# Two of four long blocks take 128 + 32 rows in the expert part of a top-k attention and mixture kernel

## The chip, the cores and the metric

The kernel runs on one core of one Trainium2 chip. Its time is the device time of one execution in microseconds. It was run three times for the figures below. The engines are TensorE (PE in the profile, its weight loads PEld), VectorE (DVE), ScalarE (ACT), GpSimd (POOL) and SyncE (SP), which issues most DMA transfers.

## The reference

Attention with top-k selection, then a mixture of experts in which each token goes to one expert and none is dropped. All numbers are fp32.

```python
# q, k, v: batch 8, heads 8, 576 tokens, head size 64; top_k = 32
scores = scale * np.matmul(q, k.transpose(0, 1, 3, 2))
kth = np.partition(scores, -top_k, axis=-1)[..., -top_k:-top_k + 1]
scores = np.where(scores >= kth, scores, -1000000000.0)
attn = softmax(scores)                     # with 1e-09 added to the sum
x = (attn @ v), laid out as (8 * 576, 8 * 64)          # 4608 x 512

logits = x @ w_gate                        # 512 x 8
expert_idx = np.argmax(logits, axis=1)
gate_w = softmax(logits) at expert_idx
# for each of the 8 experts e, with the rows that chose it:
y = np.maximum(rows @ w1[e], 0.0) @ w2[e]  # w1: 512 x 1024, w2: 1024 x 512
out = gate_w[:, None] * y                  # in the order of the tokens
```

The inputs are drawn with a fixed seed. Computed through the reference, the eight experts get 620, 519, 615, 513, 642, 507, 554 and 638 rows.

## The kernel before

The work goes batch by batch (8 batches of 576 tokens). In each, the attention of all heads is computed, the gate picks an expert for each token, and an indirect DMA (line 591) scatters the finished rows into `x_rows` in DRAM, where each expert has a region of its own. In between, the kernel takes *blocks* of rows of one expert through the two layers. Until the last batch these are full blocks of 128 rows; they are cut in pieces that are laid between the attention's instructions.

**The last part.** When the last batch is scattered, the rest is known: some full blocks and one remainder of each expert. What follows has a fixed length, written into the program: `SURE` = 2 blocks of 128 rows that are certain to be full, then `HALVES` = 4 *long* blocks, then `PLAIN` = 4 blocks of 128 rows. A long block takes a full block of an expert together with the first 64 rows (`ST`) behind it, the expert's remainder if it is 64 or less. So an expert's last full block and its short remainder share one loading of the weights, 2 MB for w1 and 2 MB for w2. Which expert a block is for is data: the program reads expert and row from a table.

**The table.** `counted` (line 699) works out for each expert the number of full blocks and a flag `half` for a remainder of at most 64. The first table (`table`, line 621) fills the two `SURE` slots. Then `end_table` (line 712) fills the long slots and the plain ones; what is left over sets `rest_i` and `rare`, which open a branch at the end of the program with spare blocks. All of that is VectorE work on one partition, on 1 to 200 numbers at a time. It uses `wTt` as scratch space. The long slots (`slot_long`) are a slice of `slot_last`. Behind the tables `fill_up` (line 606) reads each expert's end (`ends`, line 609) and writes 128 blank rows behind it (line 613), four from SP and four from GpSimd.

**The order of the work.** In the last part the instructions of PE, ACT and DVE stand in the order in which the Python code emits them. SP's queue runs in order too. Per block it holds: a read of the table and the load of the rows (`load_rows`, line 798), for a long block the load of the extra rows (`load_half`, line 812), then w1 (line 790) and w2 (line 792). At most two blocks are loaded ahead; w1 and w2 have two buffers each, so a load of w1 waits until PE has done with w1 of two blocks before.

**A long block** (`long_block`, line 872) does this on PE:

- `turned` transposes the 128 rows and the 64 rows (line 828); ACT copies both into `xT`, 4 x 192 columns (line 829).
- First layer (line 885): 8 x 4 matmuls with 128x128 weights and 192 moving columns; ACT applies the relu to four outputs at once, 768 columns (line 891).
- Between the two layers the next block's rows are transposed.
- Second layer (line 906): 8 steps of 4 matmuls with 192 columns; ACT copies the sum (line 913).
- `last` turns the result back (line 921), in two parts, 128 and 64 rows. It is put into the middle of the next block's first layer. ACT scales by the gate (line 925) and GpSimd stores the rows by an indirect DMA (line 858).

A plain block (`block`) has 32 matmuls with 128 columns in the first layer (line 949) and 8 with 512 columns in the second (line 966). The width of a long block's tiles is the constant `LONG = P + ST`, used in `spare_room` and `long_block`.

Of the kernel before, what the change touches and what calls it, by code (L numbers as in the profile page):

```python
# [9 lines left out]
F32 = mybir.dt.float32  # L10
# [34 lines left out]
def kernel(  # L45
# [82 lines left out]
    LONG = P + ST  # L128
# [95 lines left out]
    slot_long = slot_last[:, 0, NSLOT + SOON - 3 * E:].rearrange("o (i e) -> o i e", i=3)  # L224
    assert LAST - SURE <= NSLOT + SOON - 3 * E
# [473 lines left out]
    def counted():  # L699

        sm = k.small
        full, ci = sm.tile([1, E], F32, name="full"), sm.tile([1, E], I32, name="ci")
        half = wTt[0:1, 0:E]
        for to, more in ((half, P - 1), (full, ST - 1)):
            nc.vector.tensor_scalar_add(to, run[0:1, :], float(more))
            nc.vector.tensor_copy(ci, to)
            nc.vector.tensor_single_scalar(ci, ci, 7, op=ALU.arith_shift_right)
            nc.vector.tensor_copy(to, ci)
        nc.vector.tensor_tensor(half, half, full, op=ALU.subtract)
        return half, full  # L710

    def end_table(slot_i, slot_l, n, half, full):
# [4 lines left out]
        hupto, at = wTt[0:1, 3 * E:4 * E + 1], wTt[0:1, 5 * E:5 * E + NSLOT]  # L717
        long_f = wTt[0:1, 6 * E + NSLOT:9 * E + NSLOT].rearrange("o (i e) -> o i e", i=3)
# [6 lines left out]
        def looked_up(to, what, last):  # L725
            v.tensor_tensor(some[:, 0:E - 1], what[:, 1:E], what[:, 0:E - 1], op=ALU.subtract)
            v.tensor_tensor(past[:, E:2 * E, :], past[:, 0:E, :], _ins(some[:, :], 1, E), op=ALU.mult)
            v.tensor_reduce(to, past[:, E:2 * E, :], axis=AX.X, op=ALU.add)
            v.tensor_scalar(to, to, what[:, 0:1], None, ALU.add)

        def steps():
# [7 lines left out]
            v.tensor_tensor_scan(hupto[:, 1:], ones[0:1, 0:E], half, 0.0, op0=ALU.mult, op1=ALU.add)  # L739
            v.tensor_scalar(take, hupto[:, 1:], float(HALVES), None, ALU.is_le)  # L740
            v.tensor_tensor(take, take, half, op=ALU.mult)
            v.tensor_tensor(take, take, left, op=ALU.min)
            v.tensor_tensor(left, left, take, op=ALU.subtract)
# [5 lines left out]
            v.tensor_scalar(at[:, extra], slots[:, 0:HALVES], hupto[:, E:E + 1], float(EMPTY), ALU.is_lt, ALU.mult)  # L749
            v.tensor_tensor(at[:, extra], at[:, extra], slots[:, PLAIN:PLAIN + HALVES], op=ALU.add)  # L750
            v.tensor_scalar(at[:, extra], at[:, extra], hupto[:, E:E + 1], None, ALU.subtract)
# [12 lines left out]
            v.tensor_tensor(past[:, 0:E, :], _inner(slots[:, 0:E], E), _ins(hupto[:, 1:], 1, E), op=ALU.is_ge)  # L764
            v.tensor_reduce(long_f[:, 0, :], past[:, 0:E, :], axis=AX.X, op=ALU.add)
# [12 lines left out]
            v.tensor_scalar(some[:, 0:1], hupto[:, E:], float(HALVES), float(PLAIN + HALVES), ALU.min, ALU.subtract)  # L778
            v.tensor_tensor(some[:, 0:1], some[:, 0:1], upto[:, E:], op=ALU.add)
            v.tensor_scalar(some[:, 1:2], hupto[:, E:], float(-HALVES), 0.0, ALU.add, ALU.max)  # L780
# [27 lines left out]
    def load_half(n, piece):  # L808
        r = nc.sync.value_load(piece, min_val=0, max_val=EMPTY)
        room = k.att.tile([P, 2, S], F32, name="w", bufs=3)[:, :, :].rearrange("p m k -> p (m k)")  # L810
        n.half = room[:, 0:XW].rearrange("p (o w) -> p o w", o=1)
        got = nc.sync.dma_start(n.half[0:ST], xv[0:ST, bass.ds(r, 1), :]).ins
        for put in scattered:
            tc.add_manual_dep(got, put.name, WAIT)
        fetched.append(got)
        return n
# [4 lines left out]
    def turned(n):  # L821

        if hasattr(n, "half"):
            n.xT = spare_room(DT)
            for x, first, rows in ((n.x, 0, P), (n.half, P, ST)):
                ps = k.ps_m.tile([P, DT, P], F32, name="xtp", tag="m")
                for dt in range(DT):
                    nc.tensor.transpose(ps[:, dt, 0:rows], x[0:rows, 0, dt * P:(dt + 1) * P], ident[0:rows, 0:rows])
                due.append(("xT", lambda ps=ps, first=first, rows=rows: nc.scalar.copy(
                    n.xT[:, :, first:first + rows], ps[:, :, 0:rows]  # L830
                )))
            return
        if k.apart:
            ps = bank("xtp")[:, :].rearrange("p (t r) -> p t r", t=DT)
        else:
            ps = k.ps_m.tile([P, DT, P], F32, name="xtp", tag="m")
        for dt in range(DT):
            nc.tensor.transpose(ps[:, dt, :], n.x[:, 0, dt * P:(dt + 1) * P], ident)
        n.xT = k.mlp.tile([P, DT, P], F32, name="xTs")
        due.append(("xT", lambda: nc.scalar.copy(n.xT, ps)))  # L840
# [3 lines left out]
    def spare_room(n):  # L844
        flat = k.att.tile([P, 2, 2, HF], F32, name="s", bufs=4)[:, :, :, :].rearrange("p m j k -> p (m j k)")
        return flat[:, 0:n * LONG].rearrange("p (n r) -> p n r", r=LONG)
# [25 lines left out]
    def long_block(n, following):  # L872
# [6 lines left out]
        for half in range(2):  # L879
            ph = k.ps_s.tile([P, 2, SM], F32, name="sc")  # L880
            for f in range(FT // 2):
                fc = half * (FT // 2) + f
                to = ph[:, f // 2, f % 2 * LONG:(f % 2 + 1) * LONG]
                for dt in range(DT):
                    nc.tensor.matmul(
                        to, n.w1[:, 0, dt, fc * P:(fc + 1) * P], n.xT[:, dt, :],
                        start=(dt == 0), stop=(dt == DT - 1),
                    )
                if f == FT // 2 - 1:
                    hT.append(spare_room(FT // 2))  # L890
                    due.append((f"h{half}", lambda ph=ph, h=hT[half]: nc.scalar.activation(
                        h.rearrange("p (b f) r -> p b (f r)", b=2), ph[:, :, 0:2 * LONG], AF.Relu
                    )))
                yield
            if not half:
                finish()
# [4 lines left out]
        for step in range(2 * DT):  # L901
            odd, half, b = step // 4, step // 2 % 2, step % 2
            dc = 2 * b + odd
            to = pT[:, b, odd * LONG:(odd + 1) * LONG]
# [7 lines left out]
        yT = spare_room(DT)  # L912
        due.append(("y", lambda: nc.scalar.copy(
            yT.rearrange("p (b c) r -> p b (c r)", b=2), pT[:, :, 0:2 * LONG]
        )))

        def last():
            for x, first, rows in ((n.x, 0, P), (n.half, P, ST)):
# [75 lines left out]
    with fast:  # L994
# [26 lines left out]
        def ahead():  # L1021
            while waiting and len(loaded) < 2:
# [3 lines left out]
                elif isinstance(piece, list):  # L1026
                    rows_in = load_half(load_rows(SimpleNamespace(), piece[0]), piece[1])
# [53 lines left out]
        def ending(b, u):  # L1081
# [59 lines left out]
            if b == B - 1:  # L1141
                scatter(KC)
                slot_i = k.small.tile([1, 2, NSLOT], I32, name="slot_i")
                half, full = counted()
# [5 lines left out]
            if new:  # L1150
                if b == B - 1:
                    slot_i = slot_last
                    steps = end_table(slot_i, slot_long, new, half, full)
# [9 lines left out]
            if b == B - 1:  # L1163
                spare.extend(coming[PLAIN:])
                del coming[PLAIN:]
                longs = [[slot_long[0:1, i, j:j + 1] for i in range(3)] for j in range(E)]
                spare.extend((expert, half) for expert, half, _ in longs[HALVES:])
                coming[0:0] = [(expert, [full, half]) for expert, half, full in longs[:HALVES]]
# [272 lines left out]
```

## Time and profile before

| | |
|---|---|
| median of three runs | 1299.48 us (1299.31 to 1300.81) |
| the profiled execution | 1294.12 us |
| its span | 1292.5 us |
| mean granted TensorE clock | 0.97 |
| PE busy | 1185.8 us, 92% |
| DVE busy | 1057.5 us, 82% |
| ACT busy | 934.1 us, 72% |
| POOL busy | 730.1 us, 56% |
| 1075 to 1275 us: PE busy | 25.00 of 25 us in each of eight stretches |
| L885, 128x192 matmuls | 256 records, 42.8 us |
| L906, 128x192 matmuls | 256 records, 42.6 us |

The page of the profile gives each engine's busy time and a row of 40 slices of 32.3 us, each digit the busy share in tenths. The timeline lists instructions in order of time: start, duration, engine, line, operation, the tiles written and read, the form, and how many stand in a row. A PE record is given as weights and moving columns (128*128 128x192). Durations of PE records overlap, since matmuls are pipelined. Windows give busy times of all engines in a stretch. "SPq" are the issues of DMA transfers on SP's queue. Times are counted from the start of the span.

### The profile page before, as it was taken

What the parts mean: (1) busy time and instruction counts of PE and PEld (TensorE: products, weight loads), DVE (VectorE), ACT (ScalarE), POOL (GpSimd) and SP (SyncE); (2) the same over time, 40 slices, a digit from 0 to 9 for tenths busy, and PEclk for the clock granted to TensorE, in tenths of its full rate; (3) what the DMA queues carried; (4) which work ended last, traced back from release to release, by engine and by line L of the source; (5) the groups of instructions that cost most, each with busy time, mean ns of one, the idle gap of its engine ahead of it and who ended that gap; (6) DMA issues with size and microseconds to landing.
All of it is one profiled execution on the core that took longest, in us unless ns stands there. A gap on an engine that the chain in (4) does not pass through costs nothing. (4 is left out here: it accounts for less than half of the span.)

```text
span 1292.5 us, 24591 instructions
## 1 busy us (share of the span) xinstructions
PE 1185.8 (92%) x7654; PEld 835.0 (65%) x7654; DVE 1057.5 (82%) x4582; ACT 934.1 (72%) x2136; POOL 730.1 (56%) x881
## 2 busy tenths in 40 slices
PE   6776776999899999999999999999999999999998
PEld 3444444666566656676666666766666777789975
DVE  8999999999999999999999999999999954000000
ACT  4888888988898888888888888798878861112121
POOL 4777777787777765658564755585657643001010
PEclk9788888999999999999999999999999999999999
DMA  5000114731473157534755465446545558996682
GB/s 152 31 30 31 31 45 154 264 116 47 169 267 110 46 187 260 177 114 159 294 176 186 147 235 176 167 147 247 180 172 189 165 207 262 370 309 225 213 298 83
DMA packets 98798, 220.95 MB, mean 171 GB/s; under 512 B 5342, under 2 KB 26334, under 8 KB 98657
## 3 DMA queue, kind: packets, MB, share of 16 engines
q1 hardware_dynamic: 91424, 199.00, 44.9%
q0 software_dynamic: 6416, 19.97, 4.2%
q8 instruction: 62, 1.02, 0.3%
q14 instruction: 80, 0.65, 0.2%
q10 hardware_dynamic: 816, 0.31, 0.1%
HBM read 195.88 MB, written 24.17 MB: 170 GB/s over the span
## 5 line engine op out<-in xcount | busy, mean ns | idle before, releaser
L419 POOL TENSOR_TENSOR w<-s,w 128x576 f32<-128x576 f32 x288 | 407.5, 1436 | 320.6 <-ACT w L410 320.5
L949 PE MATMUL ph<-xTs,w 128*128 128x128 f32 x2112 | 261.4, 277 | 2.6 <-ACT xTs L840 2.6
L949 PEld LDWEIGHTS ph<-xTs,w 128*128 128x128 f32 x2112 | 249.7, 193 | 21.1 <-issue 17.6
L966 PE MATMUL py<-w,hT 128*128 128x512 f32 x528 | 249.5, 602 | 1.9 <-ACT hT L954 1.1
L427 ACT ACTIVATE w<-w,nbias 128x576 f32<-128x576 f32 x288 | 223.0, 785 | 2.3 <-POOL w L419 1.4
L438 PE MATMUL wTm<-turn,w 128*128 128x128 f32 x1152 | 171.4, 288 | 51.0 <-ACT oT L477 29.5
L410 ACT ACTIVATE w<-s,low 128x576 f32<-128x576 f32 x288 | 207.6, 768 | 4.7
L297 PE MATMUL sc<-qkb 64*128 64x288 f32 (+1 forms) x1280 | 200.0, 462 | 8.4 <-DMA qkb<-in_qk_dram 4.3
L438 PEld LDWEIGHTS wTm<-turn,w 128*128 128x128 f32 x1152 | 133.4, 146 | 108.9 <-ACT oT L477 37.2
L304 ACT COPY s<-sc 128x576 f32<-128x576 f32 x288 | 167.9, 634 | 11.7 <-PE sc L297 11.6
L445 ACT COPY wT<-wTm 128x512 f32<-128x512 f32 x256 | 140.5, 596 | 36.4 <-PE wTm L438 35.9
L372 DVE MAX8 tops<-scr 128x8 f32<-128x168 f32 x576 | 165.2, 314 | 0.0
L297 PEld LDWEIGHTS sc<-qkb 64*128 64x128 f32 (+1 forms) x1280 | 107.2, 190 | 72.4 <-issue 35.5
L372 DVE MAX8 tops<-few 128x8 f32<-128x144 f32 (+1 forms) x576 | 151.2, 301 | 0.0
L966 PEld LDWEIGHTS py<-w,hT 128*128 128x128 f32 x528 | 92.3, 192 | 87.1 <-issue 83.6
L475 PE MATMUL po<-wT,vb 128*64 128x288 f32 x1024 | 141.6, 420 | 0.0
L858 POOL DMA_INDIRECT out_dram<-y,xg x37 | 39.0, 1054 | 171.6 <-ACT y L975 86.2
L349 DVE MAX8 few<-l 128x8 f32<-128x288 f32 x288 | 127.0, 441 | 0.0
L313 DVE TENSOR_TENSOR h<-s 128x576 f32<-128x576 f32 (+1 forms) x145 | 110.4, 761 | 4.2 <-ACT s L304 4.2
L475 PEld LDWEIGHTS po<-wT,vb 128*64 128x64 f32 x1024 | 69.3, 140 | 67.1 <-issue 14.7
L314 DVE TENSOR_TENSOR l<-s 128x576 f32<-128x576 f32 (+1 forms) x145 | 110.8, 764 | 0.0
L349 DVE MAX8 few<-hl 128x8 f32<-128x72 f32 x576 | 99.4, 211 | 0.0
(190 smaller groups left out, 1606.3 us busy)
## 6 DMA issues: line engine op xcount, KB each, us to landing
w<-in_moe_w_dram SPq DMA_DIRECT2D x74, 2048.0 KB
qkb<-in_qk_dram SPq DMA_DIRECT2D x31, 608.0 KB
vb<-in_v_dram SPq DMA_DIRECT2D x32, 320.0 KB
xg<-x_rows SPq DMA_DIRECT2D x37, 257.0 KB
x_rows<-blank SPq DMA_DIRECT2D x13, 257.0 KB
x_rows<-blank POOLq DMA_DIRECT2D x4, 257.0 KB
x_rows<-x,posi POOLq DMA_INDIRECT x40, 3.3
out_dram<-y,xg POOLq DMA_INDIRECT x37, 4.4
```

What stands on the lines that cost most here:

```text
L297: nc.tensor.matmul(ps[rows, j, 0:HF], n.q[d, cols], n.k[d, keys], start=True, stop=True)
L304: lambda m=m, ps=ps: nc.scalar.copy(s[:, m, :, :], ps[:, :, 0:HF]) for m, ps in enumerate(got)
L349: nc.vector.max(out=f.few[:, m, QF + 8 * j:QF + 8 * j + 8], in_=away)
L372: nc.vector.max(out=tops[:, m, r * 8:(r + 1) * 8], in_=src[m])
L410: nc.scalar.activation(w[:, m, :], s[:, m, :, :].rearrange("p j k -> p (j k)"), AF.Relu, scale=-STEEP, bias=low[:, m:m + 1],)
L419: k.last_pool = in_turn(nc.gpsimd.tensor_tensor(w[:, m, :], s[:, m, :, :].rearrange("p j k -> p (j k)"), w[:, m, :], op=ALU.subtract)).ins
L427: nc.scalar.activation(w[:, m, :], w[:, m, :], AF.Exp, scale=scale, bias=nbias[:, m:m + 1], accum_out=n.z[:, c:c + 1])
L438: nc.tensor.transpose(pm[:, c * P:(c + 1) * P], w[:, m, first:first + P], ident)
L445: nc.scalar.copy(wT[:, :, m, q], pm4)
L475: nc.tensor.matmul(po[r, 0:HF], n.v[:, c, r], rhs, start=(c == 0), stop=(c == KC - 1))
L949: nc.tensor.matmul(ph[:, f, :], n.w1[:, 0, dt, fc * P:(fc + 1) * P], n.xT[:, dt, :], start=(dt == 0), stop=(dt == DT - 1),)
L966: nc.tensor.matmul(py, hT[:, f, :], n.w2[:, 0, f, :], start=(f == 0), stop=(f == FT - 1))
```

## The change

Two of the four long blocks (`BRIEF` = 2, the first two) take 128 + 32 rows; `FEW` = 32. The others stay at 128 + 64. `counted` works out a second flag, `brief`, for a remainder of at most 32. `end_table` gives the two brief slots to the first experts with that flag; their further ones count as halves and go to the other two slots. The lookup is over ten entries (`LONGS` = 8 + 2) instead of eight, in a tile of its own. `load_half` takes the number of extra rows, and `turned`, `spare_room` and `long_block` use the block's own width, 160 or 192. The spare branch gets two more blocks, as there are ten entries of which four are used.

```diff
+    BRIEF = 2
+    FEW = ST // 2
+    LONGS = E + BRIEF
...
-    slot_long = slot_last[:, 0, NSLOT + SOON - 3 * E:].rearrange("o (i e) -> o i e", i=3)
+    slot_long = const.tile([1, 3, LONGS], I32, name="slot_long")
...
-        for to, more in ((half, P - 1), (full, ST - 1)):
+        up = k.small.tile([1, E], F32, name="left")
+        for to, more in ((half, P - 1), (full, ST - 1), (up, P - FEW - 1)):
             nc.vector.tensor_scalar_add(to, run[0:1, :], float(more))
             nc.vector.tensor_copy(ci, to)
             nc.vector.tensor_single_scalar(ci, ci, 7, op=ALU.arith_shift_right)
             nc.vector.tensor_copy(to, ci)
+        nc.vector.tensor_tensor(brief, half, up, op=ALU.subtract)
         nc.vector.tensor_tensor(half, half, full, op=ALU.subtract)
...
-            v.tensor_tensor_scan(hupto[:, 1:], ones[0:1, 0:E], half, 0.0, op0=ALU.mult, op1=ALU.add)
-            v.tensor_scalar(take, hupto[:, 1:], float(HALVES), None, ALU.is_le)
+            v.tensor_tensor(brief, brief, half, op=ALU.min)
+            v.tensor_tensor_scan(bupto, ones[0:1, 0:E], brief, 0.0, op0=ALU.mult, op1=ALU.add)
+            v.tensor_scalar(take, bupto, float(BRIEF), None, ALU.is_le)
+            v.tensor_tensor(brief, brief, take, op=ALU.mult)
+            v.tensor_tensor(half, half, brief, op=ALU.subtract)
+            yield
+            v.tensor_tensor_scan(hupto, ones[0:1, 0:E], half, float(BRIEF), op0=ALU.mult, op1=ALU.add)
+            v.tensor_scalar_min(bupto, bupto, float(BRIEF))
+            v.tensor_scalar(take, hupto, float(HALVES), None, ALU.is_le)
             v.tensor_tensor(take, take, half, op=ALU.mult)
+            v.tensor_tensor(take, take, brief, op=ALU.add)
             v.tensor_tensor(take, take, left, op=ALU.min)
+            v.tensor_tensor(both, bupto[:, E - 1:E], hupto[:, E - 1:E], op=ALU.add)
...
-            v.tensor_scalar(at[:, extra], slots[:, 0:HALVES], hupto[:, E:E + 1], float(EMPTY), ALU.is_lt, ALU.mult)
-            v.tensor_tensor(at[:, extra], at[:, extra], slots[:, PLAIN:PLAIN + HALVES], op=ALU.add)
-            v.tensor_scalar(at[:, extra], at[:, extra], hupto[:, E:E + 1], None, ALU.subtract)
+            for start, stop, used, gone in ((0, BRIEF, bupto, bupto[:, E - 1:E]), (BRIEF, HALVES, hupto, both)):
+                to, first = at[:, n + start:n + stop], PLAIN + 2 * start
+                v.tensor_scalar(to, slots[:, start:stop], used[:, E - 1:E], float(EMPTY), ALU.is_lt, ALU.mult)
+                v.tensor_tensor(to, to, slots[:, first:first + stop - start], op=ALU.add)
+                v.tensor_scalar(to, to, gone, None, ALU.subtract)
...
-            v.tensor_tensor(past[:, 0:E, :], _inner(slots[:, 0:E], E), _ins(hupto[:, 1:], 1, E), op=ALU.is_ge)
-            v.tensor_reduce(long_f[:, 0, :], past[:, 0:E, :], axis=AX.X, op=ALU.add)
+            for part, used in ((slice(0, BRIEF), bupto), (slice(BRIEF, LONGS), hupto)):
+                m = part.stop - part.start
+                v.tensor_tensor(past[:, part, :], _inner(slots[:, part], E), _ins(used, 1, m), op=ALU.is_ge)
+            v.tensor_reduce(long_f[:, 0, :], past[:, 0:LONGS, :], axis=AX.X, op=ALU.add)
...
-    def load_half(n, piece):
+    def load_half(n, piece, more):
+        n.more, n.rows = more, P + more
...
-        got = nc.sync.dma_start(n.half[0:ST], xv[0:ST, bass.ds(r, 1), :]).ins
+        got = nc.sync.dma_start(n.half[0:more], xv[0:more, bass.ds(r, 1), :]).ins
...
-            n.xT = spare_room(DT)
-            for x, first, rows in ((n.x, 0, P), (n.half, P, ST)):
+            n.xT = spare_room(DT, n.rows)
+            for x, first, rows in ((n.x, 0, P), (n.half, P, n.more)):
...
-                to = ph[:, f // 2, f % 2 * LONG:(f % 2 + 1) * LONG]
+                to = ph[:, f // 2, f % 2 * n.rows:(f % 2 + 1) * n.rows]
...
-            to = pT[:, b, odd * LONG:(odd + 1) * LONG]
+            to = pT[:, b, odd * n.rows:(odd + 1) * n.rows]
...
-                longs = [[slot_long[0:1, i, j:j + 1] for i in range(3)] for j in range(E)]
+                longs = [[slot_long[0:1, i, j:j + 1] for i in range(3)] for j in range(LONGS)]
                 spare.extend((expert, half) for expert, half, _ in longs[HALVES:])
-                coming[0:0] = [(expert, [full, half]) for expert, half, full in longs[:HALVES]]
+                coming[0:0] = [
+                    (expert, [full, half, ST if j >= BRIEF else FEW])
+                    for j, (expert, half, full) in enumerate(longs[:HALVES])
+                ]
```

## The prediction

> **What bounds the kernel now.** I read the page's busy shares and its row of slices first, to see which engine ends last and where the others fall silent.
>
> ```profile
> PE 1185.8 (92%) x7654; PEld 835.0 (65%) x7654; DVE 1057.5 (82%) x4582; ACT 934.1 (72%) x2136; POOL 730.1 (56%) x881
> ...
> PE   6776776999899999999999999999999999999998
> ...
> DVE  8999999999999999999999999999999954000000
> ```
>
> The changed blocks lie in the last six slices (32.3 us each), where VectorE is silent and TensorE full. The chain of waits cannot be used here: it ends in "issue" steps of GpSimd's queue. The windows of the last part say more: the columns are the stretch, its length, busy time of PE, weight loads, DVE, ACT, POOL, the granted clock, the DMA share, GB/s.
>
> ```profile
> 1075.00:1100.00 25.00, 25.00 (x149) 18.55 (x148) 8.42 (x54) 3.64 (x6) 7.15 (x9) 1.00 1.04 318
> 1100.00:1125.00 25.00, 25.00 (x135) 17.03 (x134) 0.35 (x3) 4.12 (x7) 1.46 (x2) 1.00 1.04 381
> 1125.00:1150.00 25.00, 25.00 (x148) 20.57 (x148) 0.00 (x0) 4.52 (x8) 1.50 (x2) 1.00 1.04 368
> 1150.00:1175.00 25.00, 25.00 (x160) 24.73 (x160) 0.00 (x0) 4.90 (x9) 1.90 (x2) 1.00 0.64 212
> 1175.00:1200.00 25.00, 25.00 (x160) 24.72 (x160) 0.00 (x0) 4.31 (x7) 1.90 (x2) 1.00 0.74 253
> ```
>
> PE has no idle time at full clock, so here a nanosecond off TensorE's stream is a nanosecond off the end, unless something else becomes late. Two warnings stand in the same rows: DMA is saturated (share 1.04) up to about 1155 us, and the weight loads read as 99% busy in the long blocks.
>
> **What one matmul costs.** The timeline of PE from 1138 us on shows the blocks in a row (start, duration, line, form, count):
>
> ```profile
> 1138.42 10.56 PE L885 MATMUL sc<-s,w 128*128 128x192 f32 x64
> 1148.82 0.60 PE L828 MATMUL xtp<-turn,xg 128*128 128x128 f32 x4
> 1149.36 0.46 PE L828 MATMUL xtp<-turn,w 64*128 64x64 f32 x4
> 1149.75 10.67 PE L906 MATMUL sc<-s,w 128*128 128x192 f32 x64
> 1160.25 5.36 PE L885 MATMUL sc<-s,w 128*128 128x192 f32 x32
> ...
> 1243.10 7.31 PE L949 MATMUL ph<-xTs,w 128*128 128x128 f32 x64
> 1250.24 0.60 PE L838 MATMUL xtp<-turn,xg 128*128 128x128 f32 x4
> 1250.68 7.03 PE L966 MATMUL py<-w,hT 128*128 128x512 f32 x16
> 1257.55 7.31 PE L949 MATMUL ph<-xTs,w 128*128 128x128 f32 x64
> ```
>
> Durations overlap, so I take starts: 64 matmuls of 192 columns take 1148.82 - 1138.42 = 10.40 us, 162.5 ns each; 64 of 128 columns take 1250.24 - 1243.10 = 7.14 us, 111.6 ns; 16 of 512 columns take 6.87 us, 429.4 ns. (Each matmul in the source is two in the trace: 32 steps, 64 records.) No 160-column matmul is in the trace. Halfway between 128 and 192 lies 137.0 ns. The slope from 128 to 512 columns, 317.8 / 384 = 0.828 ns a column, taken down from 192, gives 162.5 - 32 x 0.828 = 136.0. I take 137.0, whose two rows lie nearest.
>
> **The change, part by part.**
>
> (1) Narrower matmuls. Two long blocks, each with 64 records in L885 and 64 in L906, make 2 x 128 = 256. At 162.5 - 137.0 = 25.5 ns each: 6.5 us; by the slope, 26.5 x 256 = 6.8 us. All of it lies on the path that sets the end.
>
> A rule speaks against this. The Trainium skill, "Perfetto Trace Analysis", section "Identifying the Most-Contended Engine", says to judge TensorE by how busy its weight loads are and not by its matmuls. In the long blocks they are 24.73 of 25 us busy, and the change removes no weight load: by that reading the gain would be nothing. But the 128-column phase loads one 128x128 weight for each matmul too, with a record of 192 ns (190 in the long blocks), and still starts one every 111.6 ns. So the load's own bound is at most 111.6 ns, below 137. The busy share is of overlapping records and does not bind here. Another page, "TensorE: Matmul & The Clock Gate", section "Back-to-back issue gap", prices one matmul in a stream of its own at N/2.4 + 2.5 ns. The 111.6 ns of a 128-column record are two such prices (2 x 55.8). Estimated in that way, 160 columns take 2 x (160/2.4 + 2.5) = 138.3 ns and 192 take 165.0: a gain of 26.7 ns each, 6.8 us. The rows have 162.5 where the rule has 165.0, so I keep the 25.5 between them.
>
> (2) Transposes. The four that bring in the extra rows shrink from 64x64 to 32x32 in two blocks (1149.75 - 1149.36 = 0.39 us for four). The result is between no gain and half, 0 to 0.2 us each: I take 0.05 each, 0.1 in all. Those that turn the result back (L921) still move the 128 columns of the identity at 109 ns: nothing.
>
> (3) ScalarE. L891 and L913 shrink from 768 to 640 columns, six instructions by roughly 107 ns (811 - 597 = 214 for 256 columns), L829 and L925 a little. ACT is 4.90 of 25 us busy and PE waits for it nowhere: nothing. Without that cover it would be a gain of 0.6 us.
>
> (4) Row loads and stores of half the size: 2 x 64 KB less to read of some 4 MB per block; nothing, DMA does not hold PE.
>
> (5) The table. VectorE gets 18 more instructions of 1 to 20 numbers: five in `counted`, thirteen in `end_table`. They lie between 1071.67 and 1084.45 us, and the rows around them start 0.08 to 0.39 us apart, 0.19 where one needs the last one's result:
>
> ```profile
> 1076.06 0.15 DVE L732 TENSOR_TENSOR left<-full,done 1x8 f32<-1x8 f32 x1
> 1076.25 0.15 DVE L733 TENSOR_TENSOR wTt<-wTt,left 1x8 f32<-1x8 f32 x1
> ...
> 1084.45 0.15 DVE L609 CAST ends<-run 1x8 int32<-1x8 f32 x1
> ```
>
> 18 x 0.18 = 3.2 us, so `ends` (L609) is there near 1087.8 instead of 1084.6. No VectorE work follows but three casts at 1108.9 us, behind PE. Behind `ends` wait GpSimd's four fills (first at 1087.15) and four of SP:
>
> ```profile
> 1086.55 0.35 SPq L798 DMA_DIRECT2D xg<-x_rows  x1
> 1087.70 4.62 SPq L613 DMA_DIRECT2D x_rows<-blank  x4
> 1092.56 0.41 SPq L790 DMA_DIRECT2D w<-in_moe_w_dram  x1
> ```
>
> SP is held until 1086.55 by the scatters' landing, then reads `ends` and issues 0.76 us later. In the new kernel the read cannot pass before 1087.8, so the first fill goes out near 1088.6, 0.9 us late; GpSimd's near 1.5 us late. Queued behind on SP is the w1 load of the first SURE block (1092.56), then its w2, then everything else in order. This is the tightest place of the kernel: in the landing events w1 is complete at 1108.14, and PE wants it when L966 ends at about 1108.6 us. Slack 0.5. If the 0.9 passed through whole, PE would stand still 0.4 us. It should not: the earlier weights (issued 1079.91) are landing until 1091.7, with one straggler at 1095.5, and the rings never run dry, so later fills start into a queue that is still full, and the same bytes stand ahead of w1. I take 0; bounds 0 to 1.0. The next loads have more room: w1 of the second SURE block lands at 1119.9 for 1123.4, w1 of the first long block at 1133.3 for 1138.4.
>
> (6) What becomes due earlier. From 1147 us on PE runs ahead by up to 6.6 us. Weights of the second long block land at 1146.8 and 1152.9; they are wanted at 1160.25 and 1172.45, then 3.3 and 5 us earlier: 10 and 14 us of room. Its rows land at 1141.2 for transposes at 1148.8, then at 1147.2. Later loads are issued when PE frees a buffer, so they move forward with it, and DMA is at 0.6 to 0.76 then. The order of SP's transfers is the same; only some of its register reads move. Nothing lost.
>
> Sum: 6.5 + 0.1 - 0 = 6.6 us. The profiled execution took 1294.12 us (span 1292.5, 1.6 around it) and would take 1287.5, span 1285.9. The timed runs have a median of 1299.48, 5.4 above the profiled one for a reason this trace doesn't show; the same 6.6 off gives 1292.9 us.
>
> **Rivals.** A change of 0.2% (2.6 us) is about what a measurement of this kernel can tell from none.
>
> A. *Part of the gain goes into a wait for w1* of the first SURE block. For it: slack of 0.5 us under a saturated DMA, and fills up to 1.5 us late. Against it: the full queue. At 1 to 3 us lost: 1294 to 1296, still faster.
>
> B. *DMA takes the gain whole.* For it: share 1.04 for 80 us. Against it: the narrower blocks start where that ends, and each wait I can find has 5 us or more. Then about 1299.5, no change.
>
> C. *Slower*: the longer table itself. Each of the 18 instructions would have to cost some 0.9 us or more (one instruction of this part, L538, does take 1.01), 16 us together. Then the fills come 13 to 14 us late, the queue runs dry, w1 follows by that much less some 2 us of backlog, and PE stands 11 us: less the gain, 1304. It decides from a wait of 6.6 us on. The 40 like rows at 0.15 to 0.35 us speak against it.
>
> D. *The change does not do what it says.* The seeded inputs, computed through the reference, leave remainders 108, 7, 103, 1, 2, 123, 42, 126: four experts at 64 or less, three of these at 32 or less. So the brief blocks take experts 1 and 3, the other two 4 and 6; as many plain blocks are left as before and the spare branch stays shut. And the width is written into the program: the time doesn't depend on who fills it. A weight load that did bind would be here too: 1299.5.
>
> **How the numbers follow.** Full gain 0.84 (likeliest: 1291.5 to 1294), A 0.09, B and D 0.05 together, C 0.02. Predicted 1292.9. The range reaches from 1290.8 (6.8 + 0.4 us of transposes, with 1.5 of scatter in the runs, which lay between 1299.31 and 1300.81) to 1295.5, most of A. Faster 0.93, same 0.05, slower 0.02.
>
> **What would show it.** Right: two phases of 64 at 160 columns, 8.8 us each instead of 10.4 to 10.5, in two blocks; no PE idle from 1075 us to the end; the last matmul near 1279 instead of 1286 us; `ends` near 1087.8. Wrong: spacing of 160 columns above 145 ns; a gap on PE before the L949 phase at 1108.8 (A); gaps at later L885 or L949 phases (B).

## The result and the profile after

The changed kernel takes 1292.23 us (median; 1289.86 to 1292.85), the kernel before, run beside it, 1299.39 us (1298.65 to 1300.81). The ratio is 0.994, with a 95% interval of 0.9923 to 0.9957: 7.2 us faster, by the interval 5.6 to 10. The forecast was 1292.9.

The profiled execution took 1292.85 us, with a span of 1291.2. That is only 1.3 us below the profiled execution of before. The change itself is worth more, as the next rows show. From the page of the kernel after, the busy shares and the row of slices:

```profile
PE 1182.6 (92%) x7654; PEld 831.0 (64%) x7654; DVE 1064.5 (82%) x4600; ACT 933.7 (72%) x2136; POOL 729.8 (57%) x881
...
PE   6667767899889999999999999999999999999998
...
DVE  8999999999999999999999999999999965000000
```

The number of TensorE instructions is unchanged, VectorE has the 18 more (4600 for 4582), and the picture is the same: the end belongs to TensorE. The windows of the last part of the kernel after (stretch, length, busy time of PE, weight loads, DVE, ACT, POOL, granted clock, DMA share, GB/s):

```profile
1075.00:1100.00 25.00, 25.00 (x135) 17.35 (x135) 14.34 (x95) 4.34 (x9) 8.12 (x11) 1.00 0.91 291
1100.00:1125.00 25.00, 23.83 (x152) 18.18 (x151) 0.35 (x3) 4.03 (x7) 1.97 (x2) 1.00 1.03 339
1125.00:1150.00 25.00, 25.00 (x142) 18.46 (x141) 0.00 (x0) 4.01 (x7) 1.96 (x2) 1.00 1.04 386
1150.00:1175.00 25.00, 25.00 (x189) 24.51 (x188) 0.00 (x0) 5.33 (x10) 1.64 (x2) 1.00 0.77 269
1175.00:1200.00 25.00, 25.00 (x168) 24.67 (x168) 0.00 (x0) 4.20 (x7) 2.10 (x3) 1.00 0.81 274
```

One number is new: PE is busy for 23.83 of 25 us in the second row. The timeline of PE shows where the other 1.17 us went, and the new blocks behind it (start, duration, line, form, count, and in brackets the idle time before and what ended it):

```profile
1106.33 7.03 PE L988 MATMUL py<-w,hT 128*128 128x512 f32 x16
1113.29 0.19 PE L1335 MATMUL pd<-ones,any_p 128*1 128x1 f32 x2
1114.65 7.41 PE L971 MATMUL ph<-xTs,w 128*128 128x128 f32 x64 [1.17 <-DMA w<-in_moe_w_dram]
...
1144.21 8.86 PE L907 MATMUL sc<-s,w 128*128 128x160 f32 x64
1152.90 0.60 PE L850 MATMUL xtp<-turn,xg 128*128 128x128 f32 x4
1153.44 0.43 PE L850 MATMUL xtp<-turn,w 32*128 32x32 f32 x4
1153.80 8.96 PE L928 MATMUL sc<-s,w 128*128 128x160 f32 x64
...
1278.06 7.03 PE L988 MATMUL py<-w,hT 128*128 128x512 f32 x16
```

**The new blocks.** 64 records of 160 columns take 1152.90 - 1144.21 = 8.69 us, 135.8 ns each (before: 10.40 us, 162.5 ns). The second phase of a brief block takes 8.80 us where it took 10.50. The four small transposes take 0.36 us for 0.39.

**The gap.** A matmul of one column (L1335; L1310 before) stands right ahead of the first `SURE` block. Its first record starts at 1113.29, and that block's first phase follows only 1.36 us later. In the kernel before the two stood 0.12 us apart:

```profile
1108.71 0.19 PE L1310 MATMUL pd<-ones,any_p 128*1 128x1 f32 x2
1108.83 7.41 PE L949 MATMUL ph<-xTs,w 128*128 128x128 f32 x64
```

Counted from the second record of that matmul, 0.03 us behind the first, as in all that follows, the gap is 1.33 us after and 0.09 before. The wait is for that block's w1, the place that the prediction called the tightest.

**The rest is not the change.** The last matmul of the gate (the last of ten `rank` records of L562; L560 before) starts at 1075.01 us after and at 1070.43 before. The ten in a row, first before, then after:

```profile
1069.43 1.26 PE L560 MATMUL rank<-oh,ones 128*128 128x40 f32 x10
```

```profile
1074.01 1.26 PE L562 MATMUL rank<-oh,ones 128*128 128x40 f32 x10
```

No edit of the change touches what runs up to there, and it took 4.58 us longer in this execution. So two spans cannot be subtracted here. What can be compared is the *stretch* from the second record of the one-column matmul to the start of the last matmul: 176.84 us before, 171.18 after, 5.66 less. Add the 1.24 us of wait (1.33 - 0.09), and 6.90 of gain were made, against the forecast's 6.6 with no wait.

What was open: does the longer table cause the wait, is 160 columns on a line or on a floor, and what does the choice of two brief blocks rest on?

### The profile page after: what moved, and what is told of

It reads as the page before. It is cut to its first block, busy times and chain, and to the rows that moved or that the text cites. A ratio compares the mean times of both kernels' runs of the same rounds, so it can differ in the third digit from the quotient of the medians.

```text
span 1291.2 us, 24609 instructions
## 1 busy us (share of the span) xinstructions
PE 1182.6 (92%) x7654; PEld 831.0 (64%) x7654; DVE 1064.5 (82%) x4600; ACT 933.7 (72%) x2136; POOL 729.8 (57%) x881
## 5 line engine op out<-in xcount | busy, mean ns | idle before, releaser
L971 PEld LDWEIGHTS ph<-xTs,w 128*128 128x128 f32 x2112 | 251.1, 194 | 22.4 <-issue 17.6
L477 PE MATMUL po<-wT,vb 128*64 128x288 f32 x1024 | 144.6, 427 | 0.0
```

The costliest lines, as they stand in the source:

```text
L477: nc.tensor.matmul(po[r, 0:HF], n.v[:, c, r], rhs, start=(c == 0), stop=(c == KC - 1))
L971: nc.tensor.matmul(ph[:, f, :], n.w1[:, 0, dt, fc * P:(fc + 1) * P], n.xT[:, dt, :], start=(dt == 0), stop=(dt == DT - 1),)
```

## The experiments

All traces but the two with three brief blocks, in one table; the names are those of the runs in the sections below. The second column counts from the start of the span, the columns from `ends` to "w1 complete" from the start of the gate's last matmul, all in us. `ends` is the start of the cast that gives the fills (the writes of blank rows) their addresses; w1 is the load of the first `SURE` block, which TensorE wants at about 38.3. It is complete with the last of the sixteen landing events that the trace holds for it. The gap is from the second record of the one-column matmul to the next phase: 0.09 to 0.11 is no wait.

| trace | gate's last matmul at | `ends` | first fill SP / POOL | w1 complete | gap | stretch |
|---|---|---|---|---|---|---|
| before | 1070.43 | 14.01 | 17.27 / 16.72 | 37.71 | 0.09 | 176.84 |
| before_again | 1075.00 | 14.00 | 17.29 / 16.74 | 38.28 | 0.09 | 176.83 |
| width_only | 1075.07 | 14.02 | 17.71 / 17.16 | 38.77 | 0.50 | 170.36 |
| table_only | 1075.99 | 16.82 | 17.75 / 18.75 | 38.37 | 0.11 | 176.85 |
| table_only_again | 1074.38 | 16.79 | 17.72 / 18.72 | 38.82 | 0.56 | 177.29 |
| after | 1075.01 | 16.82 | 17.75 / 18.74 | 39.59 | 1.33 | 171.18 |
| after_again | 1074.12 | 16.79 | 17.72 / 18.71 | 38.53 | 0.26 | 170.12 |
| after_third | 1076.15 | 16.79 | 17.72 / 18.72 | 39.27 | 1.01 | 170.86 |
| early_ends | 1071.53 | 1.24 | 25.83 / 17.11 | 39.37 | 1.11 | 170.97 |
| w1_first | 1073.30 | 1.24 | 27.62 / 17.97 | 34.48 | 0.09 | 169.95 |
| table_longer | 1074.84 | 20.12 | 21.04 / 22.05 | 33.36 | 0.09 | 169.95 |
| eight_rows | 1075.73 | 16.81 | 18.19 / 18.74 | 38.81 | 0.55 | 165.24 |

The stretch obeys one equation in every row: 176.84 or 169.95, by the widths, plus what the gap exceeds 0.09 to 0.11. For example 170.86 - 0.92 = 169.94 and 177.29 - 0.47 = 176.82. Nothing else in TensorE's last 180 us varies.

### The widths alone

The table of the kernel before is kept (no `brief` in `counted` or `end_table`), and the long blocks get the change's widths (width_only). For these inputs the first two long slots go to experts with 5 and 1 rows left, so that 32 rows are enough; how these remainders come about is told under "Three brief blocks".

```diff
-                coming[0:0] = [(expert, [full, half]) for expert, half, full in longs[:HALVES]]
+                coming[0:0] = [
+                    (expert, [full, half, ST if j >= BRIEF else FEW])
+                    for j, (expert, half, full) in enumerate(longs[:HALVES])
+                ]
```

> The two narrow blocks with the table of the kernel before (for these inputs its first two long slots hold experts 1 and 3, with remainders 7 and 1, so the result is whole). Theory, width and table act separately: 160 columns at 135.8 ns, from the one-column probe to the start of the last phase 163.5 us (170.4 less 6.9), no wait for w1 of the first SURE block (gap after the probe 0.1 to 0.3 us), ratio to before 0.9947. Rival, the wait is chance in that transfer and not the table's: a gap of some 1 us is as likely here as in the changed kernel. Rival, the table costs nothing: the same time as the changed kernel, ratio 0.994.

Measured: 1291.25 us (1286.6 to 1293.67), ratio 0.9962 (0.9948 to 0.9975; a ratio is estimated from all executions and is not the quotient of the medians). The stretch is 170.36, and without its wait 169.95. The timeline of PE of this kernel:

```profile
1113.35 0.19 PE L1316 MATMUL pd<-ones,any_p 128*1 128x1 f32 x2
1113.88 2.39 PE L952 MATMUL ph<-xTs,w 128*128 128x128 f32 x19 [0.34 <-DMA w<-in_moe_w_dram]
```

The kernel before took 1297.01 us (1290.7 to 1301.92, 52 executions) beside this kernel, table_only, early_ends and w1_first. The widths carry the whole gain. And the wait for w1 is here too, 0.4 us, although `ends` comes as early as before (14.02): the longer table is not needed for it.

### The table alone

The table of the change stays, and all four long blocks keep 64 rows (table_only).

```diff
-                    (expert, [full, half, ST if j >= BRIEF else FEW])
+                    (expert, [full, half, ST])
```

> The longer table with all four long blocks at 192 columns. Theory: ends comes 2.8 us later than before, measured from the same gate; w1 lands some 2 us later and PE waits for it, gap 1.2 to 1.5 us after the probe; the rest as before; ratio 1.001 (1.2 of 1299 us). Rival, chance: gap 0.1 to 0.3 us, ratio 1.000.

Measured: 1298.02 us (1293.78 to 1299.53), ratio 1.001 (0.9996 to 1.0025): no difference. The timeline of PE of this kernel:

```profile
1114.27 0.19 PE L1335 MATMUL pd<-ones,any_p 128*1 128x1 f32 x2
1114.40 2.83 PE L971 MATMUL ph<-xTs,w 128*128 128x128 f32 x23
```

`ends` and the fills are exactly as late as in the changed kernel (16.82; 17.75 and 18.75), and there is no wait: w1 was complete at 38.37. So the chain "longer table, later fills, w1 later by a fixed 1.2 us" falls.

### The same kernels once more

The kernels before and after unchanged, then after and table_only unchanged.

> The kernel before, unchanged, a second trace. If the landing of w1 of the first SURE block varies by chance from one execution to the next, it lies anywhere from 37.7 to 39.6 us after the gate's last matmul (first trace 37.7) and the gap after the probe anywhere from 0.1 to 1.3 us. If the first trace is typical: 37.7 within 0.3, gap 0.1.

> The changed kernel, a second trace. Chance: landing of w1 anywhere from 37.7 to 39.6 us after the gate's last matmul, gap 0.1 to 1.3 us. The table as the cause: 39.6 within 0.3 again, gap 1.2. The two narrow blocks take 8.7 + 8.8 us in any case, and from the end of the gap to the start of the last matmul it is 169.85 us as in the first trace.

> The changed kernel, a third trace, for the spread of w1's landing. Chance: between 37.7 and 39.6 us after the gate's last matmul. Table as the cause: the mean of the traces with the longer table stays above that of those without (38.8 against 38.25 so far, three and four traces) and this one lies above 38.4.

> The longer table with four blocks of 192 columns, a second trace, for the same spread. Chance: landing of w1 between 37.7 and 39.6, gap 0.1 to 1.3 us. Table as the cause: above 38.4, gap above 0.15.

Measured, one time each: 1298.54 us (before_again), 1290.97 (after_again), 1293.66 (after_third), 1298.38 (table_only_again). The waits of the changed kernel were 1.24, 0.17 and 0.92 us in its three traces; those of table_only 0.0 and 0.5. From the timelines of PE, first before_again, then after_again:

```profile
1113.28 0.19 PE L1310 MATMUL pd<-ones,any_p 128*1 128x1 f32 x2
1113.40 2.83 PE L949 MATMUL ph<-xTs,w 128*128 128x128 f32 x23
```

```profile
1112.40 0.19 PE L1335 MATMUL pd<-ones,any_p 128*1 128x1 f32 x2
1112.69 3.50 PE L971 MATMUL ph<-xTs,w 128*128 128x128 f32 x29
```

The kernel before had 0.5 us of slack in its first trace and none to speak of in its second (w1 complete at 38.28). The same 2 MB, behind the same transfers, come in at 37.7 or 38.3 in one kernel and at 38.5 to 39.6 in the other. With the longer table and the fills ahead of w1 (six traces) the mean is 38.90, without the longer table (three) 38.25. The ranges overlap, 38.37 to 39.59 and 37.71 to 38.77, so a shift of some 0.6 us by the table is possible and not shown. The landing events add something here: the fifteenth of the sixteen comes at a mean of 37.99 with the longer table and 37.93 without. So nearly all of w1 is there equally early, and the 0.6 us lie in the last event, which follows the fifteenth by 0.3 to 1.3 us in the first group and by 0.2 to 0.5 in the second.

The other number that moves is the start of the gate's last matmul: 1070.4 and 1075.0 for the same kernel before. The spans of the two, 1292.5 and 1296.9 us, differ by as much. A start part like the second one would make up most of the 5.4 us by which the profiled execution of before lay under its runs' median.

Where these 4.6 us arise can be read from the two traces, set side by side instruction by instruction. On ScalarE the second is 2.2 us behind at 198 us and 5.7 at 243; from 525 us on it stays 4.6 behind to the end, within 0.1. The windows of before, then of before_again:

```profile
200.00:300.00 100.00, 83.90 (x579) 56.54 (x576) 100.00 (x441) 87.11 (x202) 73.23 (x91) 0.97 0.49 172
```

```profile
200.00:300.00 100.00, 83.82 (x569) 56.98 (x566) 99.76 (x444) 84.24 (x196) 72.66 (x88) 0.93 0.49 172
```

The granted clock is 0.97 in one and 0.93 in the other; from 500 us on it is 1.00 in both. The three traces of the changed kernel, too, part before 525 us and keep their distance after it. That agrees with a clock that is granted differently from one execution to the next; that it is the cause was not tried.

### `ends` computed early

If late fills were the cause, early ones should take the wait away. `ends` is cast before the table instead of after it (early_ends). To keep the order of the transfers, SP's fills are put behind the load of the first `SURE` block's rows (`ready_load`), and w1 behind the fills; `AFTER` asks for an order and not for a wait. The same edit takes this load out of those that SP's fills are declared not to depend on.

```diff
+                ends = k.small.tile([1, E], I32, name="ends")
+                nc.vector.tensor_copy(ends, run[0:1, :])
...
-                fill_up()
+                fill_up(ends)
...
                 for other in fetched:
-                    tc.declare_no_dep(put, other, reason="empty rows go behind all full blocks")
+                    if other is not k.ready_load or on is not nc.sync:
+                        tc.declare_no_dep(put, other, reason="empty rows go behind all full blocks")
+                if on is nc.sync:
+                    tc.add_manual_dep(put, k.ready_load.name, AFTER)
+                    sp_fills.append(put)
...
-        nc.sync.dma_start(n.w1, w1v[:, bass.ds(e, 1), :, :])
+        w1_load = nc.sync.dma_start(n.w1, w1v[:, bass.ds(e, 1), :, :]).ins
+        if not k.exact and fills:
+            tc.add_manual_dep(w1_load, sp_fills[-1].name, AFTER)
```

> The changed kernel with the copy of ends ahead of both tables and the order of SP's transfers unchanged. Theory, the fills that wait for ends make w1 late: the fills go out as the scatters land, GpSimd's near 10 us after the scatters' last issue as before, the gap after the probe is 0.1 to 0.5 us, and the probe-to-last-phase stretch falls from 164.8 to 163.6 us; ratio to before 0.993. Rival, the wait is chance or comes from SP's queue in another way: gap as in the changed kernel, 1.2 us.

Measured: 1291.28 us (1287.16 to 1293.54), ratio 0.9966 (0.9952 to 0.9979), a gap of 1.11. But the kernel is not what it was meant to be. From the timeline of SP's queue:

```profile
1088.03 0.35 SPq L826 DMA_DIRECT2D xg<-x_rows  x1
1097.36 1.96 SPq L616 DMA_DIRECT2D x_rows<-blank  x4
1099.56 0.41 SPq L816 DMA_DIRECT2D w<-in_moe_w_dram  x1
```

With `ends` ready at 1.24, the first fill on SP left at 25.83, 8 us later than in the changed kernel. It waited 6.2 us for the row load of the first line, whose last landing event is at 1097.34: with the declaration gone, the fills wait for that load's landing and not only for its issue. w1 was issued 6 us later too (28.03 for 21.97), and still it was complete at 39.37, within the spread of the changed kernel. A queue that stays full does not explain this, since DMA fell to half while SP stood still. The windows of this kernel:

```profile
1093.00:1095.00 2.00, 2.00 (x6) 0.93 (x5) 0.00 (x0) 0.00 (x0) 0.00 (x0) 1.00 1.04 354
1095.00:1099.00 4.00, 4.00 (x35) 3.76 (x35) 0.00 (x0) 0.69 (x1) 0.00 (x0) 1.00 0.46 154
```

From issue to landing w1 took 11.3 us here and 17.6 in the changed kernel, which fits a shorter row of transfers before it at its issue. On the table's part in the wait this run says nothing.

### w1 ahead of the fills

The same early `ends`, without the edge that holds w1 behind the fills (w1_first). The planner, the step of the compilation that puts the instructions of each engine in order, then puts SP's four fills behind w1. They still wait for the row load, 7.9 us.

```diff
-        w1_load = nc.sync.dma_start(n.w1, w1v[:, bass.ds(e, 1), :, :]).ins
-        if not k.exact and fills:
-            tc.add_manual_dep(w1_load, sp_fills[-1].name, AFTER)
+        nc.sync.dma_start(n.w1, w1v[:, bass.ds(e, 1), :, :])
```

> Ends early, and w1 of the first SURE block ahead of SP's four fills (w2 behind them). Theory: 1 MB less of fills stands ahead of w1, it lands 2 to 5 us before PE wants it, gap 0.1 us whatever the fills do; probe to last phase 163.5 us; ratio to before 0.993, the same as with ends early alone or 0.3 us better. Rival, DMA is behind in bytes and not in order: then w2 or the next block's w1 is late instead and a gap of about 1 us shows at a later phase.

From the timelines of SP's queue and of PE of this kernel:

```profile
1090.67 0.35 SPq L823 DMA_DIRECT2D xg<-x_rows  x1
1092.43 0.37 SPq L815 DMA_DIRECT2D w<-in_moe_w_dram  x1
1100.92 2.09 SPq L616 DMA_DIRECT2D x_rows<-blank  x4
```

```profile
1111.58 0.19 PE L1342 MATMUL pd<-ones,any_p 128*1 128x1 f32 x2
1111.70 5.51 PE L975 MATMUL ph<-xTs,w 128*128 128x128 f32 x47
```

w1 is issued at 19.13 (21.97 in the changed kernel) and complete at 34.48, 3.2 us or more before any trace with SP's fills ahead of it, and the wait is gone; the stretch is 169.95, the whole gain of 6.89 us. Timed, it is 1290.67 us (1286.86 to 1291.19), ratio 0.995 (0.9934 to 0.9966). That is the best version of the change by its trace. The timed runs don't show it: the changed kernel was not timed beside it, the interval overlaps that of early_ends, which was, and a wait of a mean 0.8 us is smaller than the spread of the part before it.

Four fills of 257 KB would be half of a w1 load. That they weigh more agrees with a window of the changed kernel, just behind their issue, where DMA is as busy as around it and moves about half as much:

```profile
1099.00:1105.00 6.00, 6.00 (x57) 6.00 (x55) 0.00 (x0) 1.23 (x2) 1.04 (x1) 1.00 1.06 172
```

Share 1.06 at 172 GB/s, where the whole of 1100 to 1125 us has 1.03 at 339. In w1_first, where SP's fills leave from 1100.92 on, the same time is fast and the slow part comes later:

```profile
1099.00:1105.00 6.00, 6.00 (x53) 5.81 (x53) 0.00 (x0) 1.22 (x3) 0.71 (x1) 1.00 1.03 360
1105.00:1109.00 4.00, 4.00 (x11) 1.80 (x10) 0.00 (x0) 0.45 (x1) 0.31 (x1) 1.00 1.08 240
```

So in these two the slow part comes when the fills do.

### A table twice as late

Eighteen more one-row instructions on VectorE ahead of `ends`, which change nothing (table_longer).

```diff
+        if not k.exact:
+            for _ in range(18):
+                nc.vector.tensor_scalar_add(done, done, 0.0)
         ends = k.small.tile([1, E], I32, name="ends")
```

> The changed kernel with another 18 VectorE instructions in front of ends, each waiting for the last: ends some 3.4 us later, at 20.2 us after the gate's last matmul instead of 16.8, the first fill at 21.0 instead of 17.75. The table as the cause of the wait: w1 lands 2.5 to 3.5 us later, near 42.5 to 43, gap 3.5 to 4.5 us. A full queue that hides the fills' lateness: landing 38 to 40, gap 0.1 to 1.5 us as before.

Measured, one execution: 1291.46 us, no wait. From the timeline of SP's queue:

```profile
1091.64 0.35 SPq L822 DMA_DIRECT2D xg<-x_rows  x1
1092.23 1.10 SPq L814 DMA_DIRECT2D w<-in_moe_w_dram  x1
1095.88 0.38 SPq L618 DMA_DIRECT2D x_rows<-blank  x1
```

`ends` is 3.3 us later again (20.12 for 16.8), and the planner answered by putting w1 ahead of SP's fills, by itself. It landed at 33.36. The run is no test of a later table with the order kept; it shows a second time what the order is worth.

### Eight rows instead of 32

```diff
-    FEW = ST // 2
+    FEW = ST // 8
```

> The brief blocks take 8 extra rows (136 columns; the remainders that go there are 7 and 1). By the slope of 0.828 ns a column the start-to-start time is 116.0 ns, two blocks gain a further 2 x 128 x 19.9 ns = 5.1 us[...]. If the weight loads set a floor above 128 columns, 125 ns or more, and the gain is 2.5 us or less.

Measured, one execution: 1287.67 us (before beside it: 1296.42), stretch 165.24 with a wait of 0.46, so 164.78 without. The timeline of PE:

```profile
1144.13 7.58 PE L907 MATMUL sc<-s,w 128*128 128x136 f32 x64
1151.55 0.60 PE L850 MATMUL xtp<-turn,xg 128*128 128x128 f32 x4
...
1152.42 7.68 PE L928 MATMUL sc<-s,w 128*128 128x136 f32 x64
```

64 records in 7.42 us, 115.8 ns each. From 160 columns that is 20.0 ns for 24 columns, 0.833 ns a column; from 192 to 160 it is 0.834, and from 512 to 192 too. So from 136 columns up the time lies on one line, and there is no floor from the weight loads between 136 and 192. The 128-column row stands off it: the line gives 115.8 - 8 x 0.833 = 109.1 ns there, and 111.6 were measured. Whether a floor begins at that point was not tried. 256 x 20.0 = 5.1 us, and the stretch without its wait fell by 5.17. (The rows that go to the brief blocks are 5 and 1 and not 7 and 1; the next section says why.)

### Three brief blocks

w1_first with `BRIEF` at 3 (three_brief); then with eight rows as well (three_eight).

```diff
-    BRIEF = 2
+    BRIEF = 3
```

> Three brief blocks of 160 columns instead of two (for these inputs the remainders 7, 1 and 2; the one of 42 takes the last long block), with ends early and w1 of the first SURE block ahead of SP's fills. No wait after the probe (gap 0.1 us); from the probe to the start of the last matmul 169.95 us of w1_first less 128 x 26.7 ns = 3.4: 166.5 us. Ratio to before 176.84 - 166.5 = 10.3 us of 1297, 0.992. If the earlier blocks only moved a wait to a later load, a gap shows at a later phase and the stretch stays above 168.

> As three_brief with 8 extra rows in place of 32 (136 columns; fitted to the remainders of these inputs). At 115.8 ns as in eight_rows against 135.8: 3 x 128 x 20 ns = 7.7 us less, and some 0.2 us of transposes: probe to last matmul 158.7 us, ratio to before 0.986. If DMA becomes the bound at that pace, gaps at later phases: 160 us or more.

Measured: three_brief 1687.46 us (1685.51 to 1688.93), ratio 1.3022 (1.2991 to 1.3052); three_eight 1681.62 (1676.37 to 1683.09), ratio 1.2968 (1.2934 to 1.3001). Both are some 390 us slower than the kernel before, where a gain was expected. The timeline of PE of three_brief:

```profile
1271.46 7.03 PE L992 MATMUL py<-w,hT 128*128 128x512 f32 x16
1278.33 0.60 PE L864 MATMUL xtp<-turn,xg 128*128 128x128 f32 x4
1280.27 7.41 PE L975 MATMUL ph<-xTs,w 128*128 128x128 f32 x64 [1.34 <-ACT xTs L866]
```

The third brief block did what its width says: from the one-column matmul (1111.40) to the start of the last phase of the regular part (1271.46) and 15 matmuls of 429.3 ns more are 166.5 us, 3.4 under 169.95, as expected. In three_eight the same count gives 158.8 for the 158.7 expected, with no wait for a load. Both have w1 ahead of SP's fills: it is complete at 34.07 and 33.57, and the gap is 0.09. But where the program should end, it goes on with the spare branch, for about 400 us. The windows of the same kernel, deep in that branch:

```profile
1350.00:1500.00 150.00, 134.22 (x755) 95.74 (x754) 0.00 (x0) 20.87 (x37) 8.79 (x9) 1.00 0.77 267
1500.00:1685.00 185.00, 159.95 (x886) 112.87 (x884) 0.00 (x0) 25.29 (x43) 10.75 (x11) 0.99 0.71 247
```

So the choice of two brief blocks and two of 64 rows can't be moved freely. Why the branch opens follows from working the tables through for these inputs; the run itself shows only that it opens. After the first batch `filled_up` (with `SOON` = 3) pads the three largest experts to full blocks: experts 0, 1 and 4 get 25, 49 and 32 blank rows. Worked out with these, the remainders at the end are 5, 56, 103, 1, 34, 123, 42 and 126. Expert 1's last full block is already taken when the table is made, so that its 56 rows take a plain block, as do the remainders of experts 2, 5 and 7. The brief slots go to experts 0 and 3 (5 and 1 rows), the 64-row slots to 4 and 6 (34 and 42). With three brief slots one of them stays without a remainder, and only one 64-row slot is left for two experts: expert 6's rows remain over, `rest_i` becomes 1, and the branch runs. What was expected of the run had the wrong remainders (7, 1 and 2 for the brief slots). The changed kernel fits these inputs with no 64-row slot to spare.

## Why the prediction was right, point by point

**(1) Narrower matmuls: right.** 137.0 ns were taken for a record of 160 columns, from the rows on both sides; 135.8 were measured, and the slope (136.0), the alternative that was not taken, was nearer. Halfway was 1.2 too high because the 128-column row itself stands 2.5 above the line through 136, 160, 192 and 512 columns. Two phases save 1.71 and 1.70 us in each of two blocks, 6.82 us together for the 6.5 forecast. The warning on weight loads did not come true: they still read 24.51 and 24.67 of 25 us, after the change as before, and the time per matmul followed the columns down to 115.8 ns at 136. (The page that the warning came from names the share of the peak FLOP/s beside the weight loads' share; the prediction left that out.) The price by the Trainium skill, "TensorE: Matmul & The Clock Gate", section "Back-to-back issue gap", which the prediction worked out as 138.3 ns for 160 columns, is 2.5 above the measured 135.8; for 136 columns the same sum gives 118.3 for 115.8, and 165.0 for 162.5 at 192. It is high by 2.5 ns at all three, so that differences come out right; only at 128 columns, where the prediction checked it, does it fit (111.7 for 111.6). Counted once in a record and not twice, the page's 2.5 ns gives as an estimate 2 x N/2.4 + 2.5: 115.8, 135.8 and 162.5, as measured, and 429.2 for the 429.4 at 512. The section gives this price for a matmul alone. For a stream of weight loads and matmuls it has about 81 ns at 128 columns and 131 at 512; taken twice, 162 and 262, these do not fit the 111.6 and 429.4 here.

**(2) Transposes: right, nothing in it.** 0.03 us a block for the 0.05 taken.

**(3) and (4) ScalarE and the row loads: right.** PE waits for neither in the last part; the one wait there is w1's.

**(5) The table: right in its own size; the 0 for PE's wait was the mis-sized term.** 18 instructions took 2.8 us (`ends` at 16.8 instead of 14.0) for the 3.2 forecast, SP's first fill is 0.48 late for 0.9, GpSimd's 2.0 for 1.5. The prediction took 0 for what PE would wait, with bounds of 0 to 1.0. PE waited 1.24, 0.17 and 0.92 us in three traces, 0.8 in the mean and once beyond the bound. What failed is the reading of slack from one trace. "Slack 0.5" was a figure of one execution; in another of the same kernel it was 0.1, and the landing of w1 moves by up to 1 us between executions of one kernel. Whether the longer table adds to this is open: 0.6 us between the means, all of it in the last of sixteen landing events, ranges that overlap, and a wait of 0.4 us without it (width_only).

**(6) What becomes due earlier: right.** No wait follows w1's in any trace of the table, and the stretch repeats to 0.02 us.

**The sum.** 6.6 was forecast. Without the wait it is 176.84 - 169.95 = 6.89 (6.82 from the phases and 0.06 from transposes); with the waits of the three traces it is 5.66, 6.72 and 5.98, mean 6.1. The difference of the timed medians, 7.2 with an interval of 5.6 to 10, holds both. That the forecast lay so near the median is partly chance: the two errors have opposite signs, 0.3 too little for the columns and 0.8 too little for the wait, and the median of the runs carries the several us by which the start of the last part moves. The 7.2 come from four executions of each kernel. Of the 52 executions of the kernel before that were timed later, 12 lie under 1292 us, below the median of the changed kernel. Against their median of 1297.01 the three kernels with the same widths gain 5.7 to 6.3 us by their own medians.

**The rivals.** A came true in part: the place and the wait are the ones it named, at 0.2 to 1.2 us and not 1 to 3. B and C did not happen: no other wait, and 0.16 us for an instruction of the table (2.8 / 18). D's verdict was right and its account wrong. It took remainders from the reference's counts and left out the blank rows of `filled_up`; it named experts 1 and 3 for the brief blocks, and they are 0 and 3. "Four experts at 64 or less, three of these at 32 or less" would have let a third brief block in, and three_brief shows what that costs: 392 us over the kernel before beside it.

**The signs named in advance.** Two phases of 64 at 160 columns, 8.8 us each: there (8.69 and 8.80). No PE idle: wrong, 1.17 us. The last matmul near 1279: it starts 6.4 us into the phase of 1278.06, near 1284.5. The last part began 4.58 us later than in the trace that the 1279 was counted from; less that, it is 1279.9. `ends` near 1087.8: there by the same count (16.82 us and the 0.15 of the cast behind 1070.43 is 1087.4).

## What to carry to other kernels

Where an engine's stream sets the end and starts follow each other without gaps, count a change from start-to-start times on both sides of the new size; a weight-load share of 98% or more was no floor here, down to 136 columns. Compare two traces from a common event near the change, not by their spans, and read slack at a transfer in a full queue from several executions: one trace's 0.5 us was 0.1 in the next. And when a table picks blocks by data, follow the data through every step that pads or moves rows before saying that one more slot can be narrowed.

## What was not expected of the hardware

- **Behind the fills DMA is slow.** For some 6 us behind their issue DMA reads as busy as ever (1.06) and moves 172 GB/s, about half of the 339 to 386 around; in w1_first the slow part comes later, as the fills do. Putting one 2 MB load ahead of four of them brought it in 3 us or more earlier (34.48 and 33.36 for 37.7 to 39.6). Whether the fills themselves are what is slow, or what is read behind them, was not tried.
- **A transfer's landing moves by 1 us with nothing changed.** w1 of the changed kernel: 38.53, 39.27, 39.59 us after the same event. Fifteen of its sixteen landing events are in by 38.01 to 38.53; the last one makes the rest. TensorE's own stretch repeats to 0.02 us.
- **The part before moves more than the change is worth.** The gate's last matmul starts between 1070.4 and 1076.2 us in the twelve traces of the table, and at both 1070.4 and 1075.0 for one kernel. In the traces compared, the difference arises before 525 us, where the granted clock is below 1 and not the same in each.
- **Edits of the order did something else than was meant.** With `ends` 15 us earlier SP's first fill came 8 us later, since it now waited for a load that the same edit no longer excepted; and 18 idle instructions put w1 ahead of the fills. Issue order and waits have to be read from the new trace before a run is taken as a test.
